# Layer-0 backward w1 blocks in four transfers each with sums in natural order, fewer output units inside the turn, and a new order of the last output units

## The chip, the cores and the metric

The kernel runs on one core of one Trainium2 chip. The metric is the device time of one execution in microseconds; the median of three runs before the change is 1110.19 us (1109.47 to 1112.6).

A core has five engines that run their own instruction streams in order and wait for each other on semaphores: PE (TensorE, matmuls), DVE (VectorE), ACT (ScalarE), POOL (GpSimd) and SP (SyncE). Here SP issues all loads from device memory, and the output row `out_1`; POOL issues nearly all stores. Sixteen DMA engines move the bytes for both.

## The reference

A decode step for a batch of 2 rows: two layers of grouped-query attention over a cached K and V of 16384 positions, each followed by an MLP, with the same weights in both layers, and the gradients of all inputs but `B_x`.

```python
def _A_ref(x, k_cache, v_cache, wq, wo):          # B=2, Hq=32, Hkv=4, Sk=16384, Dh=128, D=1024
    q = (x @ wq).reshape(B, Sq, Hq, Dh).transpose(0, 2, 1, 3)
    k, v = repeat(k_cache, 8, axis=1), repeat(v_cache, 8, axis=1)
    p = softmax(einsum("bhqd,bhkd->bhqk", q, k) * Dh ** -0.5)
    return einsum("bhqk,bhkd->bhqd", p, v).transpose(0, 2, 1, 3).reshape(B, Sq, Hq * Dh) @ wo
def _B_ref(x, w1, b1, w2, b2):                    # w1: 1024 x 3584, w2: 3584 x 1024
    return gelu(layernorm(x) @ w1 + b1) @ w2 + b2
x = x + _A_ref(layernorm(x), ...)                 # layer 0
x = x + _B_ref(layernorm(x), ...)
x = x + _A_ref(layernorm(x), ...)                 # layer 1, same weights
x = x + _B_ref(layernorm(x), ...)
# outputs: x and, by vjp(grad_out), the gradients of A_x, k_cache, v_cache, wq, wo, w1, b1, w2, b2
```

All tensors are bfloat16. K, V and their gradients are 32 MB each (8 pairs of batch row and KV head, 16384 x 128), `wq` and `wo` 8 MB each, `w1` and `w2` 7 MB each.

## The kernel before

K and V are read in pieces of 1 MB (32 positions of each of 128 partitions) and weights in blocks of 896 KB or 1 MB, into 16 slots of 1 MB in SBUF and a few regions that are free for a time. A recording layer (`Program`) collects the pieces of work in the order in which they are emitted, each with the chunks that it uses, and then places each load as early as a slot is free; so SP's queue holds the loads in the order of their first use, and a load waits there until the last reader of its slot is done. Each load also takes one of eight completion semaphores in turn, so that it waits until the load eight places ahead has landed.

The order of stages is: attention and MLP forward of layer 0, the same of layer 1, MLP backward of layer 1, attention backward of layer 1 (`attn_bwd(1, ...)`), **the turn** (MLP backward of layer 0), attention backward of layer 0 (`attn_bwd(0, ...)`), and **the end**. All large outputs are computed from the turn on: the weight gradients and the K and V gradients are outer products of a few rows, each unit of output being one matmul into a 128 x 512 PSUM bank, one cast into a staging slot by ACT or DVE (`cast_out`, L276 and L279), and after four or eight units one store from POOL's queue (L1333 for weights, 512 KB; L1257 for K and V, 1 MB).

The turn, by its emitted order (L1490 to L1530):

- `here_products` with w2 (PE L465, 224 matmuls) give dh; DVE multiplies it by the GELU slope (L1504), and `spread` (PE L506, DVE L507) lays it out for the products with w1.
- w1 comes in 8 blocks `ws1c` of 512 rows x 896 columns (`ld_rows`, L378), four row groups of 128 side by side in a partition: partition p of group j holds row 128j + p. `turn_rows` turns each block in 32 x 32 squares with two DVE instructions (L437). The list `t1` holds these 16 turns; its first two are placed in the last steps of `attn_bwd(1)`, the next two behind it, five between the products with w2, and the rest behind `spread`.
- `p1`, for each block 28 matmuls (PE L487), adds to `dm_0`, 128 x 16 in bank `sb[0]`. Because of the turning in squares the sums come out with partition groups of 32 and row groups exchanged, so that `unquad` copies them to natural order: one DVE copy out of PSUM (L517) and 16 copies of 32 partitions over DVE, ACT and POOL (L525 to L529, pattern `on="vag"`).
- Between the blocks of `p1` stand the first nine pieces of `first`: rows and columns for the w2 gradient (`y_rows`, `x_rows`) and its first six units. Six more units (`first[9:15]`) stand between the layer norm's sums (`g1p[0]`: DVE L649 to L652, PE L594) and the rest of it (`g1p[1]`: DVE L657 to L929).
- The result `gA_all` feeds the products with wo (PE L465, 64 matmuls) and `do_of`, after which `attn_bwd(0)` starts with its first V chunk (DVE L537).

`unquad` also serves `wo_bwd_ops` (three times in layer 0) and the MLP backward of layer 1; `dn_kept` and `dh_last_` call it with POOL alone.

In `attn_bwd`, `direct` adds the products of each K chunk to the query gradient in `sb[0][:, 0:8]` (PE L575); `dq_of` reads it out and clears it (L1052, L1054) once per position.

The end is written out by hand in `todo` (L1155 to L1158). What is left then: `dq_of` of the last position, 16 units and one turn (`turn`, PE L1233, copied at L1240 or L1243) of the last K gradient, a `y_rows`, eight groups of products with wq (`tail`, PE L465), the layer norm's backward (`sums` and `rest` in `attn_in_bwd`), the row `out_1` (L617 to L619), and 16 units of the wq gradient.

```python
todo = ev.pop(s) + kv_units[0:2] + rows + tail[0:4] + kv_units[2:4] + tail[4:] + units[0:2] + parts[0:1]
todo += units[2:5] + parts[1:2] + units[5:9] + parts[2:] + kv_units[4:] + units[9:]
```

Of the kernel before, what the change touches and what calls it, by code (L numbers as in the profile page):

```python
# [29 lines left out]
N_END = 133  # L30
# [152 lines left out]
def kernel(  # L183
# [24 lines left out]
    nc = tc.nc  # L208
# [38 lines left out]
    def flat(t):  # L247
        return t.rearrange("p a b -> p (a b)")
# [33 lines left out]
    def dve(us):  # L282
        load_of("dve", us)
# [92 lines left out]
    def ld_rows(nm, W, j0, rb, c0, n):  # L376
# [3 lines left out]
            W[j0 * 128:(j0 + rb) * 128, c0:c0 + n].rearrange("(j p) n -> p j n", p=128)), (nm, j0, c0))  # L380

    def ld_wq(k):
        return [ld_rows("wq", A_wq, 4 * i, 4, k * 1024, 1024) for i in range(2)]
# [128 lines left out]

    def unquad(dst, src, on="vag"):

        C = src.shape[1]
        q = small.tile([128, 8, 4, 2], F32, name="uq", bufs=1)[:, 0:C]
        V.tensor_copy(out=q, in_=src)  # L517
        n = 0
        for a in range(4):
            for j in range(4):  # L520
                d, s_ = dst[32 * a:32 * a + 32, :, j], q[32 * j:32 * j + 32, :, a]
                e = on[n % len(on)]
                n += 1
                if e == "v":
                    V.tensor_copy(out=d, in_=s_)  # L525
                elif e == "a":
                    S.copy(out=d, in_=s_)
                else:
                    GP.tensor_copy(out=d, in_=s_)  # L529
# [116 lines left out]

    def ln_bwd_sums(dy, y, at=None):
        t1 = wrk.tile([128, DJ, 2], F32, name="lb_t1")
        V.tensor_tensor(out=t1[:], in0=dy, in1=y, op=ALU.mult)  # L649
        s = small.tile([128, 2, 2], F32, name="lb_s")  # L650
        V.tensor_reduce(out=s[:, 0, :], in_=dy.rearrange("p j b -> p b j"), axis=AX.X, op=ALU.add)
        V.tensor_reduce(out=s[:, 1, :], in_=t1[:].rearrange("p j b -> p b j"), axis=AX.X, op=ALU.add)  # L652
        return part_sum(flat(s[:]), 4, at)

# [368 lines left out]

    def attn_bwd(l, order, gT, wo_first, outputs=None, mark=None, extra=None):

# [24 lines left out]
        def dq_of(pos, g):  # L1050
            def fn():
                V.tensor_scalar(out=dq_all[:, (g % HKV) * R:(g % HKV + 1) * R, 2 * l + g // HKV], in0=sb[0][:, 0:8],  # L1052
                                scalar1=QSCALE, scalar2=None, op0=ALU.mult)
                V.memset(sb[0][:, 0:8], 0.0)  # L1054
                dve(0.3)
            return fn
# [56 lines left out]
        while s <= n_steps:  # L1113
# [5 lines left out]
            for v in k_at.get(s, ()):  # L1119
                vpos, vi = divmod(v, 16)  # L1120
                vg = order[vpos]
                if vi % 4 == 0:
                    vc[0] = ld_kv("K", vg, vi // 4)
                c = vc[0]

                def pk(vpos=vpos, vg=vg, vi=vi, c=c):
                    direct(sb[0][:, 0:8], c, vi, xt[vpos % 2], False)

                mids.append((pk, [c]))
# [21 lines left out]
        if l == 1:  # L1151
            todo = tail + parts
        else:
            rows, kv_units, units = outputs(s, True)
            todo = ev.pop(s) + kv_units[0:2] + rows + tail[0:4] + kv_units[2:4] + tail[4:] + units[0:2] + parts[0:1]  # L1155
            todo += units[2:5] + parts[1:2] + units[5:9] + parts[2:] + kv_units[4:] + units[9:]
        for b in todo:
# [3 lines left out]
    def attn_in_bwd(l, gT, dnq):  # L1161
        h = {}

        def sums():
# [6 lines left out]
            h["dn"] = dn  # L1171
            h["ps"] = ln_bwd_sums(dn[:], vec_y[f"a{l}"][:], half[0, 0] if l == 1 else sb[0][:, 200:])
            dve(0.8)

        def rest():
# [6 lines left out]

        res = [(sums, ()), (rest, ())]
        if l == 0:
# [4 lines left out]
    def kv_outputs(pos, g):  # L1189
# [30 lines left out]
        for c, w in [(c, w) for c in range(NCH) for w in (1, 0)]:  # L1220
            at_ = base + 4 * c + 4 * (pos == 0) if w == 1 else base + 14 + 4 * c
            if w == 0 and pos == G - 1:
                at_ = (124, 127, N_END + 1, N_END + 3)[c]
            stg = P.chunk(kind="full")
# [21 lines left out]

            res.append((at_ - 2, turn, ()))
            for u in range(8):
# [229 lines left out]

    ws1c = [ld_rows("w1q", B_w1, 4 * h, 4, cg * 896, 896) for h in range(2) for cg in range(4)]
    dm_0 = quads(at_sb0(224, 16))  # L1480
    vh0, spread_h0 = spread(lambda: dh_all[:, :, 0:2], FJ, "vh")
# [7 lines left out]
    extra[30] = [col_to_row(xM1, out_0.rearrange("b s d -> (b s) d"), kind="load")]  # L1489
    attn_bwd(1, up, lambda: saved["g3"], (None, wo_prods), mark=mark("d1"), extra=extra)  # L1490
    wo_prods0 = wo_first_ops(0, down[0] % HKV, saved["wo"])[2]


    g2 = saved["gA1"]
    for b in t1[2:4]:
        emit(*b)
# [18 lines left out]
    first = [y_rows(gM_all, 0, 8, 0, 0)] + dw_units("h", 0, 0, pieces_rows(out_8, F, D))  # L1515
    rest_h = first[15:]
    for n, b in enumerate(p1):
        emit(*b)
        for u in first[n + (n > 0):n + 2]:
            emit(*u)  # L1520
    va0, spread_a0 = spread(lambda: gA_all[:, :, 0:2], DJ, "va")
    g1p = mlp_in_bwd(0, lambda dm: unquad(dm[:].rearrange("p (c j) b -> p c j b", j=4), dm_0), g2, parts=True)
    emit(g1p[0])
    emit(lambda: load_of("dve", 6.0))
    for u in first[9:15]:
        emit(*u)
# [93 lines left out]
```

## Time and profile before

| What | Before |
|---|---|
| median of 3 runs | 1110.19 us (1109.47 to 1112.6) |
| the profiled execution, its own time | 1110.15 us |
| its span from first to last instruction | 1108.4 us |
| mean granted TensorE clock | 0.821 |
| busy: PE, DVE, ACT, POOL | 815.9, 761.3, 493.1, 182.6 us (74%, 69%, 44%, 16%) |
| read, written | 349.20 MB, 98.62 MB |
| DMA busy share and rate, 675 to 730 us | 0.97, 375 GB/s |
| DMA busy share and rate, 730 to 1086 us | 1.02, 419 GB/s |
| DMA busy share and rate, 1086 to 1099 us | 0.49, 200 GB/s |

The spans of the stages are read from the timeline: the turn lies between about 641 us, when the last K chunk of layer 1's backward is used, and 675 us, when layer 0's attention backward turns its first V chunk; the last store is issued at 1099.59 us. The DMA share is the mean over the 16 engines of the time in which a packet was under way; it goes a little above 1 where packets overlap, so that 1.0 means that all sixteen always had work.

### The profile page before, as it was taken

Reading aid. Unit: us, or ns where it says so; the run is one execution under the profiler, and the core shown is the slowest. Engines: PE = TensorE matmul, PEld = TensorE weight load, DVE = VectorE, ACT = ScalarE, POOL = GpSimd, SP = SyncE. Lnnn points to the kernel's source line nnn. Section 1 sums busy time; section 2 is a strip of 40 time slices with the busy share of each in tenths; the row PEclk is TensorE's granted clock in tenths of the full one; section 3 lists DMA queues with packets and bytes.
Section 4 is the critical chain, followed back from the end, with each engine's and each line's share of the span. In section 5 each row is a group of like instructions: output and inputs, shape, how many; then the busy total and the mean of one; then the engine's idle time right before and its main releaser. Section 6 shows DMA issues by size and latency. Waiting matters only on the chain. (4 is left out here: it accounts for less than half of the span.)

```text
span 1108.4 us, 34192 instructions
## 1 busy us (share of the span) xinstructions
PE 815.9 (74%) x14689; PEld 609.3 (55%) x14689; DVE 761.3 (69%) x1474; ACT 493.1 (44%) x1133; POOL 182.6 (16%) x577
## 2 busy tenths in 40 slices
PE   5665666456888647888778678878876896698895
PEld 4554555455777547777677564444443443344453
DVE  5864665169888627665546476979776895598984
ACT  0322222102233222235434326767665785487874
POOL 1000000001000000111111101423332332233431
PEclk9999999997555555569868657999897998699998
DMA  9999999999999998999999989999999999999996
GB/s 372 421 422 421 422 425 421 398 404 399 418 423 421 422 421 345 409 419 421 419 423 416 417 318 411 355 399 422 420 420 425 423 419 422 420 402 421 410 423 250
DMA packets 97448, 450.03 MB, mean 406 GB/s; under 512 B 7528, under 2 KB 11638, under 8 KB 58512
## 3 DMA queue, kind: packets, MB, share of 16 engines
q1 hardware_dynamic: 79504, 349.22, 77.3%
q0 software_dynamic: 17792, 98.62, 21.6%
q8 instruction: 115, 1.88, 0.6%
q14 instruction: 37, 0.30, 0.1%
HBM read 349.20 MB, written 98.62 MB: 404 GB/s over the span
## 5 line engine op out<-in xcount | busy, mean ns | idle before, releaser
L537 DVE STREAM_TRANSPOSE kT<-slot 128x512 int32<-128x512 int32 x420 | 283.1, 694 | 112.8 <-PE sc L550 90.2
L550 PE MATMUL sc<-qbd,kT 128*128 128x32 bf16 x4096 | 262.5, 222 | 12.6 <-DVE kT L537 11.0
L550 PEld LDWEIGHTS <-kT 128*128 128x128 bf16 x4096 | 209.1, 115 | 64.7 <-issue 32.9
L575 PEld LDWEIGHTS <-slot 128*128 128x128 bf16 x3520 | 143.9, 103 | 106.7 <-issue 47.1
L575 PE MATMUL sb<-xt,slot 128*128 128x8 bf16 x3520 | 161.1, 176 | 49.0 <-DMA slot<-in_A_v_cache_dram 22.9
L276 ACT CAST slot<-sc 128x512 bf16<-128x512 f32 x293 | 167.0, 592 | 60.4 <-PE sc L1307 38.0
L1252 PE MATMUL sc<-slot,late 128*128 128x512 bf16 x350 | 131.1, 397 | 17.7 <-DVE slot L279 5.7
L279 DVE CAST slot<-sc 128x512 bf16<-128x512 f32 x171 | 114.3, 677 | 27.5 <-PE sc L1252 14.2
L760 ACT ACTIVATE e<-sc 128x512 bf16<-128x512 f32 x32 | 19.0, 597 | 235.9 <-DVE sc L757 169.0
L276 ACT CAST slot<-sb 128x512 bf16<-128x512 f32 x139 | 82.4, 593 | 37.1 <-PE sb L1307 17.0
L455 ACT COPY slot<-tp 128x512 int32<-128x512 int32 x88 | 50.3, 587 | 103.7 <-PE tp L452 103.4
L452 PE MATMUL tp<-ident,slot 128*128 128x128 bf16 x768 | 71.3, 255 | 13.2 <-ACT slot L455 6.0
L1252 PEld LDWEIGHTS <-late 128*128 128x128 bf16 x512 | 44.7, 98 | 62.2 <-issue 48.7
L585 ACT COPY xt<-e 32x128 int32<-32x128 int32 x256 | 75.6, 295 | 3.9
L1252 PE MATMUL sb<-slot,late 128*128 128x512 bf16 x162 | 65.6, 405 | 12.6 <-DVE slot L279 7.7
L1307 PE MATMUL sc<-slot,late 128*128 128x512 bf16 x159 | 64.0, 424 | 11.3 <-DVE e L279 6.2
L437 DVE STREAM_TRANSPOSE slot<-slot 128x1024 int32<-128x1024 int32 (+1 forms) x48 | 55.2, 1176 | 17.0 <-DMA slot<-in_A_wo_dram 8.0
L452 PEld LDWEIGHTS <-slot 128*128 128x128 bf16 x768 | 58.0, 116 | 15.9 <-issue 6.8
L279 DVE CAST slot<-sb 128x512 bf16<-128x512 f32 x81 | 54.9, 678 | 9.7 <-PE sb L1307 4.3
L642 POOL TENSOR_TENSOR m_rstd<-ln_vpe,neghalf 128x2 f32<-128x2 f32 x2 | 1.4, 715 | 349.6 <-DVE ln_vpe L640 349.6
L585 POOL COPY xt<-late 32x64 int32<-32x64 int32 x240 | 55.2, 230 | 13.0 <-DVE late L1046 1.9
L585 POOL COPY xt<-ds 32x64 int32<-32x64 int32 x128 | 29.5, 231 | 159.6 <-DVE ds L1046 104.7
(303 smaller groups left out, 1104.4 us busy)
## 6 DMA issues: line engine op xcount, KB each, us to landing
slot<-in_A_k_cache_dram SPq DMA_DIRECT2D x105, 1024.0 KB, 17.3
slot<-in_A_v_cache_dram SPq DMA_DIRECT2D x98, 1024.0 KB, 17.9
out_dram<-slot POOLq DMA_DIRECT2D x57, 1024.0 KB, 14.6
slot<-in_A_wq_dram SPq DMA_DIRECT2D x25, 1024.0 KB, 16.7
slot<-in_A_wo_dram SPq DMA_DIRECT2D x25, 1024.0 KB, 19.7
out_dram<-slot POOLq DMA_DIRECT2D x43, 512.0 KB, 13.9
slot<-in_B_w_dram SPq DMA_DIRECT2D x23, 896.0 KB, 15.4
slot<-in_B_w_dram SPq DMA_DIRECT2D x12, 1024.0 KB, 13.2
```

The source lines that it names most:

```text
L276: S.copy(out=dst, in_=src)
L279: V.tensor_copy(out=dst, in_=src)
L437: V.transpose(out=t.ap[:, h * nw * 256:(h + 1) * nw * 256].bitcast(I32).rearrange("p (w j m) -> p w j m", j=4, m=32), in_=c.ap[:, 0:4 * nc ...
L452: PE.transpose(tp[:, j * 128:(j + 1) * 128], c.ap[:, off + j * 128:off + (j + 1) * 128], ident[:])
L455: S.copy(out=d.bitcast(I32), in_=tp.bitcast(I32))
L537: V.transpose(out=kT[:].bitcast(I32).rearrange("p (w j m) -> p w j m", w=4, j=4), in_=c.ap[:, (i % 4) * 1024:(i % 4 + 1) * 1024].bitcast(I ...
L550: PE.matmul(sc[:, a0:a0 + 4, :, 2 * (i % 4) + q], lhsT=kv[:, 2 * q + w, :, e], rhs=qbd[:, q_at(g), 2 * w + e], start=(w == 0 and e == 0), ...
L575: PE.matmul(acc, lhsT=c.ap[:, n * 128:(n + 1) * 128], rhs=xv[:, i // 4, t // 2, :, 2 * (i % 4) + t % 2], start=(fresh and i == 0 and t == ...
L585: (GP.tensor_copy if on[t % len(on)] == "g" else S.copy)(out=d[32 * t:32 * t + 32, c0:c0 + cn, j, :], in_=s[32 * j:32 * j + 32, c0:c0 + cn ...
L760: S.activation(out=e_of(l, g)[:, 8 * f:8 * f + 8].rearrange("p a h b -> p h a b"), in_=sc[f][:].rearrange("p h (a b) -> p h a b", b=8), fu ...
L1252: PE.matmul(ps, lhsT=hold["blk"][:, j, :], rhs=flat(qm(w)[:, (u % 2) * 4:(u % 2) * 4 + 4, :]), start=True, stop=True)
L1307: PE.matmul(ps, lhsT=hold[j // 4 * 4][:, j % 4, :], rhs=Y.ap[:, y_at + c0:y_at + c0 + cn], start=True, stop=True)
```

## The change

It has five parts.

1. `ld_quads` takes the place of `ld_rows` for the eight w1 blocks of the turn: four transfers for each block, one for each row group j, each into all 128 partitions (1792 bytes a row, 224 KB). Partition 32a + r of group j now holds row 128a + 32j + r. On the memory side a transfer's access pattern is 4 x 32 x 896 (a, r, columns; strides 458752, 3584 and 1 elements), on the SBUF side 128 x 896; before, it was 128 x 4 x 896 on both sides. In the built program each transfer takes a completion semaphore of its own, and the order of SP's queue is otherwise as it was.
2. The sums then stand in natural order, and one DVE copy takes the place of `unquad` there. The other users of `unquad` get the pattern `vgvagvvg`: 8 copies on DVE, 6 on POOL, 2 on ACT, where it was 6, 5 and 5.
3. Two of the nine pieces of `first` stay inside `p1` (a `y_rows` behind the fourth block, an `x_rows` behind the sixth), and four units instead of six between the two parts of the layer norm. Eight units (two stores of 512 KB) move to the background of `attn_bwd(0)`. One turn of the second block moves ahead of layer 1's last layer norm (`mid`).
4. The query gradient of `attn_bwd` is added up in two places in turn, so that a position's products do not share the columns that the one before is read from.
5. At the end the last turn of the K gradient moves into the loop, the layer norm's sums are split from their matmul (`close`), and the units stand in another order.

```diff
+    def ld_quads(nm, W, j0, c0, n):
+
+        def load(ap):
+            src = W[j0 * 128:(j0 + 4) * 128, c0:c0 + n].rearrange("(a j r) n -> j a r n", a=4, j=4)
+            for j in range(4):
+                nc.sync.dma_start(ap[:, j * n:(j + 1) * n], src[j])
+
+        return P.chunk(load, (nm, j0, c0))
...
-    def unquad(dst, src, on="vag"):
+    def unquad(dst, src, on="vgvagvvg"):
...
-    def ln_bwd_sums(dy, y, at=None):
+    def ln_bwd_terms(dy, y):
...
-        return part_sum(flat(s[:]), 4, at)
+        return flat(s[:])
+
+    def ln_bwd_sums(dy, y, at=None):
+        return part_sum(ln_bwd_terms(dy, y), 4, at)
...
-                V.tensor_scalar(out=dq_all[:, (g % HKV) * R:(g % HKV + 1) * R, 2 * l + g // HKV], in0=sb[0][:, 0:8],
+                acc = sb[0][:, pos % 2 * 8:pos % 2 * 8 + 8]
+                V.tensor_scalar(out=dq_all[:, (g % HKV) * R:(g % HKV + 1) * R, 2 * l + g // HKV], in0=acc,
                                 scalar1=QSCALE, scalar2=None, op0=ALU.mult)
-                V.memset(sb[0][:, 0:8], 0.0)
+                V.memset(acc, 0.0)
...
-                    direct(sb[0][:, 0:8], c, vi, xt[vpos % 2], False)
+                    direct(sb[0][:, vpos % 2 * 8:vpos % 2 * 8 + 8], c, vi, xt[vpos % 2], False)
...
-            todo = tail + parts
+            todo = tail + list(mid) + parts
...
-            todo = ev.pop(s) + kv_units[0:2] + rows + tail[0:4] + kv_units[2:4] + tail[4:] + units[0:2] + parts[0:1]
-            todo += units[2:5] + parts[1:2] + units[5:9] + parts[2:] + kv_units[4:] + units[9:]
+            todo = ev.pop(s) + kv_units[0:4] + rows + kv_units[4:6] + tail[0:4] + kv_units[6:8] + tail[4:] + kv_units[8:10]
+            todo += parts[0:1] + units[0:4] + parts[1:2] + units[4:8] + parts[2:3] + kv_units[10:13] + parts[3:]
+            todo += kv_units[13:] + units[8:]
...
-            h["ps"] = ln_bwd_sums(dn[:], vec_y[f"a{l}"][:], half[0, 0] if l == 1 else sb[0][:, 200:])
+            h["s"] = ln_bwd_terms(dn[:], vec_y[f"a{l}"][:])
             dve(0.8)
+
+        def close():
+            h["ps"] = part_sum(h["s"], 4, half[0, 0] if l == 1 else sb[0][:, 200:])
...
-        res = [(sums, ()), (rest, ())]
+        res = [(sums, ()), (close, ()), (rest, ())]
...
-                at_ = (124, 127, N_END + 1, N_END + 3)[c]
+                at_ = (124, 127, N_END + 1, N_END + 2)[c]
...
-            res.append((at_ - 2, turn, ()))
+            res.append((min(at_ - 2, N_END - 1), turn, ()))
...
-    ws1c = [ld_rows("w1q", B_w1, 4 * h, 4, cg * 896, 896) for h in range(2) for cg in range(4)]
-    dm_0 = quads(at_sb0(224, 16))
+    ws1c = [ld_quads("w1q", B_w1, 4 * h, cg * 896, 896) for h in range(2) for cg in range(4)]
+    dm_0 = at_sb0(224, 16).rearrange("p (c a b) -> p c a b", a=4, b=2)
...
-    attn_bwd(1, up, lambda: saved["g3"], (None, wo_prods), mark=mark("d1"), extra=extra)
+    attn_bwd(1, up, lambda: saved["g3"], (None, wo_prods), mark=mark("d1"), extra=extra, mid=t1[2:3])
...
-    for b in t1[2:4]:
+    for b in t1[3:4]:
         emit(*b)
...
-    rest_h = first[15:]
+    rest_h = first[6:]
     for n, b in enumerate(p1):
         emit(*b)
-        for u in first[n + (n > 0):n + 2]:
-            emit(*u)
+        if n in (3, 5):
+            emit(*first[n // 4])
...
-    g1p = mlp_in_bwd(0, lambda dm: unquad(dm[:].rearrange("p (c j) b -> p c j b", j=4), dm_0), g2, parts=True)
+    g1p = mlp_in_bwd(0, lambda dm: V.tensor_copy(out=dm[:], in_=dm_0.rearrange("p c a b -> p (c a) b")), g2, parts=True)
...
-    for u in first[9:15]:
+    for u in first[2:6]:
         emit(*u)
```

More of the change, by code (lines that the diff above doesn't have):

```diff
@@ L1022, in wq_last_ops, with attn_bwd @@
         return turns, prods
-    def attn_bwd(l, order, gT, wo_first, outputs=None, mark=None, extra=None):
+    def attn_bwd(l, order, gT, wo_first, outputs=None, mark=None, extra=None, mid=()):
         kvs = []
```

## The prediction

> **What bounds the kernel now.** I read the stages' DMA share first, then the DMA issues and packets, then the timelines of the turn and of the end.
>
> ```profile
> 642.00:645.00 3.00, 1.94 (x53) 1.79 (x51) 0.86 (x6) 0.00 (x0) 0.52 (x1) 0.50 1.04 388
> ...
> 660.00:663.00 3.00, 3.00 (x84) 2.41 (x82) 2.25 (x3) 1.72 (x3) 0.00 (x0) 0.50 0.09 33
> ...
> 730.00:1086.00 356.00, 291.95 (x3545) 157.61 (x3545) 280.60 (x481) 248.78 (x496) 118.16 (x349) 0.92 1.02 419
> ```
>
> The last three columns of these windows are granted clock, DMA share and GB/s. Over most of the span the sixteen DMA engines are full at about 420 GB/s; what is lost is lost in gaps, such as 660 to 663 us inside the turn (33 GB/s). So an edit is worth what it takes from a gap, and a new gap costs its full length. While the w1 blocks land (642 to 645) the engines are full too, at 388 GB/s.
>
> ```profile
> DMA packets 97448, 450.03 MB, mean 406 GB/s; under 512 B 7528, under 2 KB 11638, under 8 KB 58512
> ## 3 DMA queue, kind: packets, MB, share of 16 engines
> q1 hardware_dynamic: 79504, 349.22, 77.3%
> ```
>
> ```profile
> e<-in_A_x_dram SPq DMA_DIRECT2D x1, 4.0 KB
> ds<-in_grad_out_dram SPq DMA_DIRECT2D x1, 4.0 KB
> ds<-in_B_b_dram SPq DMA_DIRECT2D x1, 7.0 KB
> slot<-in_B_b_dram SPq DMA_DIRECT2D x1, 2.0 KB
> ```
>
> These tell on how many engines a transfer of SP's queue runs. By the list of issues the queue carries 239 K and V chunks of 128 rows, 73 weight blocks of 512 rows (wq 31, wo 28, w2 14), 16 forward w1 blocks of 128 rows, 8 w1 blocks of 512 rows for the turn, and five small transfers with 2, 2, 1, 1 and 2 rows (the four shown and the row `out_1`). One packet a row makes 30592 + 37376 + 2048 + 4096 + 8 = 74120. The queue has 79504; the other 5384 are exactly 336 x 16 + 8. So each of the 336 large transfers, whose outermost dimension is 128, has 16 extra packets, and the five small ones have 8, which is their rows 2+2+1+1+2. I read the extra packet as one completion for each engine that took part: a transfer uses no more engines than its outermost dimension has entries.
>
> ```profile
> 660.18 2.11 DVE L437 STREAM_TRANSPOSE slot<-slot 128x896 int32<-128x896 int32 x2
> 665.38 0.17 DVE L517 COPY uq<-sb 128x16 f32<-128x16 f32 x1 [3.09 <-PE sb L487]
> 665.59 1.04 DVE L525 COPY dm_sb<-uq 32x4 f32<-32x4 f32 x6
> 667.53 0.17 DVE L649 TENSOR_TENSOR lb_t<-dm_sb,m_y 128x16 f32<-128x16 f32 x1 [0.90 <-ACT dm_sb L527]
> ...
> 675.09 1.27 DVE L537 STREAM_TRANSPOSE kT<-slot 128x512 int32<-128x512 int32 x2
> ```
>
> This is the chain of the turn: the last block's turning, its products on PE (waited for 3.09 us), the copying to natural order, the layer norm, the first V chunk.
>
> **The change part by part.**
>
> *The four transfers.* On the SBUF side each has 128 entries outermost, as all large ones have; on the memory side it has 4. The trace has no transfer whose sides differ. A part that one engine moves must be cut on both sides, and a cut along the outermost dimensions that both share gives four parts; so I take four engines. The bounds are 16 engines (no loss) and four. [...]
>
> One transfer on four engines gives each 57344 bytes, as much as a whole block gives each of sixteen, so it takes what a block took.
>
> ```profile
> slot<-in_B_w_dram SPq DMA_DIRECT2D x1, 896.0 KB, 10.7
> ...
> slot<-in_B_w_dram SPq DMA_DIRECT2D x1, 896.0 KB, 12.3
> ```
>
> These are the second and third block, issued at 631.55 and 632.18 us by SP's timeline: landed at 642.25 and 644.48, 2.2 us apart; 917504 bytes at the 388 GB/s of the window above are 2.36. I take 2.3 us (bounds 2.18, at 420 GB/s, and 2.45, at 375). The first block landed at 637.5 (issued 625.24, 12.3). Now three steps more: 644.4. Behind it stands a K chunk, 2.5 us: 646.9. Then 28 transfers, 64.4 us: the last lands at 711.3, where it was 656.1 (649.60 + 6.5). Only eight may be under way, but all eight stand on the same four engines (18 us of work), so SP's issues (0.38 us each, 32 for 8) and waits are hidden behind them; twelve engines idle. SP's later loads are queued behind these. Turning the last block takes 2.11 us, its 28 products 0.94 (PE L487 in the timeline): the sums are read at 714.4 instead of 665.38, +49.0. In between, the half-turn moved into `mid` makes DVE wait for the second block (landing at 656), and with it the last layer norm of layer 1 and the w2 products; all of that ends before 670 and hides behind the loads. With 16 engines it costs nothing, as DVE idles 1.94 us there.
>
> *Natural order.* From L517 to L649 were 2.15 us; one copy of 0.17 and its hand-over leave 0.2: -1.95. It is on the chain in either case.
>
> *Fewer units.* Seven units less among the products would let them end with the turning (below, 3.0 us); behind the loads this is worth nothing. Four units instead of six behind the sums: PE came to the wo products at 671.03, while `gA_all` was written at 670.21: -0.8. Eight units and two stores (1 MB) move into attention backward: 2.5 us at 419 GB/s where the engines are full, nothing where they fill the 6 us that 675 to 730 loses at 375 GB/s: +1.2 (0 to 2.5).
>
> The first V chunk is turned 49.0 - 1.95 - 0.8 = 46.2 us later. Loads behind it: two V chunks are issued near 695, behind the blocks, and land within 5 us of 711; the third waits for all four transfers into its slot and for the turning, 713.4, and lands 5.0 later (as the one issued at 662.32 did), long before the twelve-odd us of work on the first two are done: 0 (to +5).
>
> *The other `unquad` users*: two DVE copies more (0.17 each), three ACT copies fewer (0.2), three times in a stage that loads bound: 0 (-1 to +1). *Two accumulators*: PE spares a wait of at most 0.4 us per position, behind the same loads: 0 (-1).
>
> *The end.*
>
> ```profile
> 1095.40 0.57 POOL L1257 DMA_DIRECT2D out_dram<-slot  x1 [2.41 <-ACT slot L276]
> ...
> 1099.59 0.74 POOL L1333 DMA_DIRECT2D out_dram<-ds  x1 [0.48 <-issue]
> ```
>
> From the clearing of the last accumulator (1083.66) to the last cast (1099.03) are 15.4 us, for 32 casts of 0.69 on DVE and 0.59 on ACT: 10.2 us side by side. DVE's other work (out-row, layer norm, 3.5) and ACT's row (1.0), shared, add 2.25: 12.4. The first K store, at 1095.40, now needs only units that stand ahead of the norm, so fewer stores queue behind each other at the end. -3 (0 to -5).
>
> Sum: 1110.15 (the profiled execution; the median, 1110.19, is the same) + 46.2 + 1.2 - 3 = **1154.5 us**.
>
> **The rivals.**
>
> *Sixteen engines after all*, or different fours for successive transfers: the SBUF side alone decides, for it the 128 partitions speak; against it, nothing in the trace but the reading above. SP issues two loads back to back 0.44 us apart (652.26 and 652.70), a transfer takes 0.57, so the rate holds. Then the last block's products start with its turning's end, 0.85 earlier because `mid` takes a turn off DVE: they end at 662.4 instead of 665.38, -3.0, and with -1.95 and -0.8 the chain gains 5.75. Of this the moved stores give back up to 2.5 and full loads from 730 on some more: -3.5. With the end's -3: **1103.6**, faster. It decides if the first block lands near 637.5.
>
> *Sixteen engines, but too few bytes under way.* Eight transfers of 224 KB are 1.79 MB; if each takes the 6.5 us from issue to landing that the last block took, plus 0.4 for the issue, the rate is 266 GB/s instead of 388, and 7.34 MB take 27.6 us instead of 18.9: +8.7. With the gains (-5.8, -3) and +1.2 for the stores: **1111.3**. Against it: a chunk issued into an empty queue (662.32) landed after 5.0 us, 2.5 of which are its own bytes.
>
> **How the numbers follow.** Four engines 0.80, sixteen 0.13, too few under way 0.07. Four engines alone span 31 steps at 2.18 to 2.45 (-3.7, +4.7), the stores, the late V chunk (+5), the end (-2, +3) and, downwards, gaps behind the turn that a delayed stage may fill (675 to 730 and 1086 to 1099 lose 6 us each): 1139 to 1168. The two rivals lie below it and hold 2 in 10. This kernel's runs scatter by 0.3%, so less than 3.3 us is no change. Faster: 0.11 of the first rival's 0.13. No change: the rest of it and half of the second, 0.05. Slower: 0.84.
>
> **What would show it.** With four engines the windows between 650 and 710 us show a DMA share of a quarter and some 100 GB/s, DVE L437 waits for the w1 loads for tens of us, and SP's queue has 79504 - 128 + 32 x 4 = 79504 packets again; with sixteen it has 79888. The first V chunk is turned near 721. L517 is gone from the turn, and L649 follows the copy by 0.2 us. At the end a K store is issued near 1088 plus the delay. I am wrong if the first block lands near 637, as before.

## The result and the profile after

| | before | after |
|---|---|---|
| median, runs of one job | 1110.68 us (1109.47 to 1112.6, 5 runs) | 1167.17 us (1166.57 to 1168.54, 5 runs) |
| the profiled execution, its own time and span | 1110.15 and 1108.4 us | 1166.57 and 1164.8 us |
| mean granted TensorE clock | 0.821 | 0.821 |

After takes 1.051 times as long as before (95% interval 1.0499 to 1.0522): +56.5 us, where +44.3 was forecast (1154.5 less 1110.19). 1167.17 lies inside the predicted range of 1139 to 1168, near its upper end.

Three windows of the trace of after. The columns are the window and its length, the busy time and (behind an x) the instructions of PE, PE's weight loads, DVE, ACT and POOL, then granted clock, DMA share and GB/s.

```profile
644.00:647.00 3.00, 1.02 (x32) 0.95 (x33) 1.29 (x4) 0.00 (x0) 0.00 (x0) 0.50 0.26 101
650.00:700.00 50.00, 13.48 (x410) 12.58 (x410) 13.56 (x24) 3.26 (x3) 0.00 (x0) 0.50 0.27 102
776.00:1145.00 369.00, 299.04 (x3608) 161.45 (x3606) 288.90 (x500) 253.86 (x499) 120.97 (x356) 0.94 1.01 415
```

While w1 lands, a quarter of the DMA engines' time is used and 102 GB/s are moved; before it was 388 GB/s in the window of the prediction, and 355 GB/s from 637 to 652 us. Later all sixteen are full again, at 415 GB/s. The page's lines on packets have the counts of before:

```profile
DMA packets 97448, 450.03 MB, mean 386 GB/s; under 512 B 7528, under 2 KB 11638, under 8 KB 58512
...
q1 hardware_dynamic: 79504, 349.22, 74.1%
```

That SP's queue has 79504 packets once more, with 24 more transfers, is the sign that the prediction named: 8 transfers with 16 extra packets each went, 32 with 4 each came.

The timelines of SP's queue and of DVE in after, through the turn:

```profile
637.21 61.65 SPq L387 DMA_DIRECT2D slot<-in_B_w_dram  x26
698.96 14.70 SPq L373 DMA_DIRECT2D slot<-in_A_v_cache_dram  x4
```

```profile
710.72 2.11 DVE L446 STREAM_TRANSPOSE slot<-slot 128x896 int32<-128x896 int32 x2 [8.78 <-DMA slot<-in_B_w_dram]
713.46 0.17 DVE L1539 COPY dm_sb<-sb 128x16 f32<-128x16 f32 x1 [0.63 <-PE sb L496]
713.66 0.17 DVE L658 TENSOR_TENSOR lb_t<-dm_sb,m_y 128x16 f32<-128x16 f32 x1
...
720.70 1.86 DVE L546 STREAM_TRANSPOSE kT<-slot 128x512 int32<-128x512 int32 x3
```

```profile
DVE slot L446 <- DMA slot<-in_B_w_dram: 51.7, 7, 9.2
```

SP issues 26 of the 32 transfers in 61.65 us; the later ones follow each other by 2.19 us: in the program each waits for the transfer eight places ahead, and 229376 bytes at the 102 GB/s of the window are 2.25. DVE waits for them seven times, 51.7 us in all (the last line: total, how often, longest), as the prediction said. The last block is turned at 710.72 (before 660.18), its sums are copied at 713.46 (before 665.38, +48.1), the layer norm follows 0.20 us behind, and the first V chunk is turned at 720.70 (before 675.09): +45.6.

The end of after, from POOL's timeline:

```profile
1147.93 0.53 POOL L1274 DMA_DIRECT2D out_dram<-slot  x1 [5.84 <-ACT slot L276]
...
1157.74 0.72 POOL L1350 DMA_DIRECT2D out_dram<-ds  x1 [0.49 <-issue]
```

The last store is issued at 1157.74 instead of 1099.59. So the delay grows from +45.6 at the first V chunk to +58.1 there, and is +56.4 at the end of the span. Read along the turnings of the K and V chunks (DVE L546, before L537), it is +47.2 at the 9th, +53.5 at the 17th, +53.2 still at the 24th from the end, and +57.8 at the 16th from the end.

One more point of the traces orders what follows. The third V load of layer 0 (in e11 the second) is the first load that goes into a slot out of which a w1 block was turned; SP issues it right behind the last block's turning (710.72 + 2.11 = 712.83 in after), and five more loads follow within 4 us. I call it **the late load**. SP's timelines of before and of after have it at 662.32 and 712.86 us (+50.5):

```profile
662.32 0.33 SPq L373 DMA_DIRECT2D slot<-in_A_v_cache_dram  x1
```

```profile
712.86 0.33 SPq L373 DMA_DIRECT2D slot<-in_A_v_cache_dram  x1
```

From it to the end of the span the kernels here move 179 MB (e11 180), which is 426 us at 420 GB/s (419 in before from 730 to 1086 us); the rest of that **stretch** is roughly what the DMA engines lose in it.

| kernel | what differs | late load, us | stretch, us | median (its range), us |
|---|---|---|---|---|
| before | | 662.3 | 446.1 | 1110.61 to 1111.51 in the jobs |
| after | | 712.9 | 451.9 | 1167.17 |
| e1 | after, 32 outermost, groups of 32 partitions | 676.5 | 452.8 | 1132.72 (1131.08 to 1136.37) |
| e2 | after, 8 outermost | 682.6 | 452.4 | 1136.62 (1136.41 to 1137.06) |
| e3 | after, units in the turn | 715.3 | 444.8 | 1161.12 (1159.24 to 1162.1) |
| e4 | before, new end | 664.0 | 446.6 | 1110.75 (1109.79 to 1112.46) |
| e5 | after, loads and sums of before | 663.7 | 455.5 | 1117.69 (1115.68 to 1121.02) |
| e6 | e5, four transfers by row groups | 664.1 | 453.2 | 1120.05 (1119.08 to 1123.64) |
| e7 | e5, four transfers by groups of 32 partitions | 678.9 | 458.2 | 1132.02 (1129.35 to 1138.88) |
| e8 | after, clearing on DVE | 713.8 | 451.8 | 1166.90 (1166.72 to 1167.43) |
| e9 | after, rate of before | 714.0 | 449.9 | 1165.74 (1164.77 to 1166.52) |
| e10 | e5, rate of before | 662.9 | 450.0 | 1115.13 (1110.35 to 1117.71) |
| e11 | e5, six staging halves | 662.3 | 449.5 | 1112.22 (1111.09 to 1113.57) |
| e12 | e5, units in the turn | 663.6 | 445.7 | 1110.76 (1108.69 to 1111.72) |

The late load and the stretch are of the profiled execution. In e4, e5, e7 and e11 that was the longest one, 1.8, 3.3, 6.9 and 1.4 us above the median, so that the two columns together are too long there by as much. Kernels with the same turn (after, e8, e9) have the late load at 712.9 to 714.0, so a difference of 1 us in that column means nothing.

### The profile page after: what moved, and what is told of

It is laid out like the page before. It is cut to its first block, busy times and chain, and to the rows that moved or that the text cites. A ratio compares the mean times of both kernels' runs of the same rounds, so it can differ in the third digit from the quotient of the medians.

```text
span 1164.8 us, 34252 instructions
## 1 busy us (share of the span) xinstructions
PE 816.7 (70%) x14689; PEld 610.6 (52%) x14689; DVE 763.9 (66%) x1480; ACT 488.0 (42%) x1112; POOL 182.4 (16%) x576
## 3 DMA queue, kind: packets, MB, share of 16 engines
q1 hardware_dynamic: 79504, 349.22, 74.1%
## 5 line engine op out<-in xcount | busy, mean ns | idle before, releaser
L546 DVE STREAM_TRANSPOSE kT<-slot 128x512 int32<-128x512 int32 x420 | 282.9, 694 | 107.9 <-PE sc L559 87.6
L276 ACT CAST slot<-sc 128x512 bf16<-128x512 f32 x274 | 156.6, 593 | 39.8 <-PE sc L1324 19.0
L1269 PE MATMUL sc<-slot,late 128*128 128x512 bf16 x336 | 126.7, 400 | 31.5 <-DVE slot L279 11.2
L279 DVE CAST slot<-sc 128x512 bf16<-128x512 f32 x182 | 121.4, 676 | 34.4 <-PE sc L1324 12.0
L276 ACT CAST slot<-sb 128x512 bf16<-128x512 f32 x154 | 91.1, 592 | 65.3 <-PE sb L1324 40.7
L446 DVE STREAM_TRANSPOSE slot<-slot 128x1024 int32<-128x1024 int32 (+1 forms) x48 | 55.4, 1177 | 59.5 <-DMA slot<-in_B_w_dram 51.7
L1269 PE MATMUL sb<-slot,late 128*128 128x512 bf16 x176 | 70.3, 400 | 8.2 <-DVE slot L279 3.9
L1324 PE MATMUL sc<-slot,late 128*128 128x512 bf16 x172 | 65.0, 404 | 7.8 <-DVE slot L279 4.0
L1350 POOL DMA_DIRECT2D out_dram<-slot x50 | 33.1, 663 | 154.1 <-DMA slot<-in_A_v_cache_dram 69.0
L279 DVE CAST slot<-sb 128x512 bf16<-128x512 f32 x70 | 47.6, 679 | 12.5 <-PE sb L1269 6.8
```

Of the source, the lines that this page charges most:

```text
L276: S.copy(out=dst, in_=src)
L279: V.tensor_copy(out=dst, in_=src)
L446: V.transpose(out=t.ap[:, h * nw * 256:(h + 1) * nw * 256].bitcast(I32).rearrange("p (w j m) -> p w j m", j=4, m=32), in_=c.ap[:, 0:4 * nc ...
L546: V.transpose(out=kT[:].bitcast(I32).rearrange("p (w j m) -> p w j m", w=4, j=4), in_=c.ap[:, (i % 4) * 1024:(i % 4 + 1) * 1024].bitcast(I ...
L1269: PE.matmul(ps, lhsT=hold["blk"][:, j, :], rhs=flat(qm(w)[:, (u % 2) * 4:(u % 2) * 4 + 4, :]), start=True, stop=True)
L1324: PE.matmul(ps, lhsT=hold[j // 4 * 4][:, j % 4, :], rhs=Y.ap[:, y_at + c0:y_at + c0 + cn], start=True, stop=True)
```

## The experiments

### What slows the loads: e1, e2, e6, e7

All four keep 32 transfers of 224 KB and the other parts of the change.

**e1**, partition groups in place of row groups, so that both sides have 32 outermost:

```diff
-            src = W[j0 * 128:(j0 + 4) * 128, c0:c0 + n].rearrange("(a j r) n -> j a r n", a=4, j=4)
-            for j in range(4):
-                nc.sync.dma_start(ap[:, j * n:(j + 1) * n], src[j])
+            src = W[j0 * 128:(j0 + 4) * 128, c0:c0 + n].rearrange("(a j r) n -> a r j n", a=4, j=4)
+            for a in range(4):
+                nc.sync.dma_start(ap[32 * a:32 * a + 32, 0:4 * n].rearrange("p (j n) -> p j n", j=4), src[a])
```

> The changed kernel, with each w1 block of the turn again in four transfers of 224 KB, sums in natural order, but cut by partition groups of 32 instead of row groups: each transfer's outermost dimension is 32 on both sides. Theory F (the outermost 4 of the memory side holds a transfer to four DMA engines): the step goes from the 2.19 us measured after the change to 0.5 to 0.6 us, the first block lands near 637.5 us, SP's queue shows 79888 packets, the windows of the turn show a DMA share near 1 again. Rival T (four small transfers for each block are slow in themselves, by too few bytes under way): the first V chunk is still turned after 678 us. On the 12 us that the changed kernel loses behind the turn: if they come from loads that start late behind the blocks (theory L), they go too, and the time is 1102 to 1108 us; if they come from the eight units and two stores moved behind the turn (theory U), they stay, and it is 1112 to 1119 us.

Measured 1132.72 us: neither of the two times. The first V chunk is turned at 684.36, behind the 678 us that rival T gave as its sign. Packets and a window, of the page and the trace of e1:

```profile
q1 hardware_dynamic: 79888, 349.22, 77.5%
```

```profile
655.00:670.00 15.00, 10.19 (x345) 9.86 (x345) 10.88 (x12) 1.90 (x1) 0.00 (x0) 0.50 1.08 235
```

All sixteen engines take part (79888 packets) and are busy all the time (share 1.08), but they move 235 GB/s; SP issues the transfers some 1.0 us apart, not the 0.5 to 0.6 expected. So the count of engines was right and was not all that matters. Whether the number of the transfers, their rows or their partitions slow them was open.

**e2**, eight outermost on the memory side:

```diff
-            src = W[j0 * 128:(j0 + 4) * 128, c0:c0 + n].rearrange("(a j r) n -> j a r n", a=4, j=4)
+            src = W[j0 * 128:(j0 + 4) * 128, c0:c0 + n].rearrange("(a j r) n -> j a r n", a=8, j=4)
```

> The changed kernel, with the memory side of the four transfers 8 x 16 x 896 instead of 4 x 32 x 896: the same bytes, the same row length, the same 128 partitions, but rows reach other partitions, so the gradients behind these products are computed from permuted sums. Theory F: eight engines, a step of 1.10 us (half of 2.19), a DMA share near a half while the blocks land, SP's queue 79504 + 32 x 4 - 0 completions less than with sixteen, that is 79632 packets; the turn ends about 16 us later than with sixteen engines (51 us x (35 - 19) / (70 - 19)), so the time is 1116 to 1128 us. If the slowness comes from the row groups or the strides and not from the count, the step stays near 2.2 us and the time near 1165 us.

Measured 1136.62 us, outside the forecast, with the mechanism as theory F has it:

```profile
q1 hardware_dynamic: 79632, 349.22, 76.1%
```

```profile
650.00:665.00 15.00, 7.08 (x241) 6.87 (x238) 8.01 (x18) 1.90 (x1) 0.03 (x1) 0.50 0.53 201
```

79632 packets, a share of half, 201 GB/s, twice the 102 of four; by that rate a transfer of 229376 bytes takes 1.14 us, where theory F had 1.10. The time was off because I added the longer turn to about 1104 us. Added to the time of the kernel with the loads and sums of before (e5, 1117.69), the delay of the late load (682.6 - 663.7 = 18.9) gives 1136.6; e5 is known to about 2 us only, so that it fits so well is in part chance. Since e2's rows reach other partitions, its gradients are other numbers, and only its time and its trace are used here.

**e6**, four transfers by row groups in the row order of before, 128 outermost on both sides (sums by `unquad` again, as in e5):

```diff
-            src = W[j0 * 128:(j0 + 4) * 128, c0:c0 + n].rearrange("(a j r) n -> j a r n", a=4, j=4)
+            src = W[j0 * 128:(j0 + 4) * 128, c0:c0 + n].rearrange("(j p) n -> j p n", j=4)
```

> As e5, but each w1 block in four transfers of 224 KB, one for each row group of 128 rows, all partitions (128 x 896 on both sides): the number, the size and the partitions of the changed kernel's transfers, without the 4 on the memory side. Theory F (the outermost 4 is what costs): the time of e5 within 3 us, the blocks land at 380 GB/s or more, SP's queue shows 79504 + 24 x 16 = 79888 packets. Rival T (four transfers of 224 KB for each block are slow in themselves, as e1 with its 1.0 us steps could mean): the blocks land at 230 to 300 GB/s, and the time is that of e5 plus 8 to 20 us.

Measured 1120.05 us, 2.4 above e5, whose range it overlaps; the late load comes 0.4 us later than in e5. SP's queue in the timeline of e6, and a window while the blocks land:

```profile
636.14 17.04 SPq L387 DMA_DIRECT2D slot<-in_B_w_dram  x25
```

```profile
642.00:657.00 15.00, 8.96 (x297) 8.56 (x294) 10.50 (x21) 1.90 (x1) 0.52 (x1) 0.50 1.00 358
```

25 transfers in 17.0 us where after had 26 in 61.65, and SP's queue has the 79888 packets of sixteen engines. 358 GB/s are less than the 380 that theory F had, but before and e5 move no more from 642 to 657 us (344 and 348). So four transfers of 224 KB for a block cost next to nothing; rival T falls, and with it the prediction's "too few bytes under way". With the same number, size and partitions, only the memory side with its 4 outermost is left to explain after; that it is their number is what e2 shows, where 8 in place of 4 double the rate (201 GB/s instead of 102).

**e7**, as e6, but cut by groups of 32 partitions:

```diff
+            for a in range(4):
+                nc.sync.dma_start(ap[32 * a:32 * a + 32, 0:4 * n].rearrange("p (j n) -> p j n", j=4), src[32 * a:32 * a + 32])
```

> As e5, but each w1 block in four transfers of 224 KB, one for each group of 32 partitions (32 x 4 x 896 on both sides), rows in the order of before. In e1 such transfers used all sixteen engines but moved only 231 to 251 GB/s. Theory N (a transfer into 32 partitions alone is slower for each packet, whatever the rows): 230 to 260 GB/s while the blocks land with a DMA share near 1, a step of 0.9 to 1.1 us, 1128 to 1138 us. If the slowness of e1 came from its row order (rows 32 apart in one partition), the blocks land at 380 GB/s or more and the time is that of e5.

Measured 1132.02 us, and in a window of e7:

```profile
657.00:672.00 15.00, 10.25 (x346) 9.91 (x346) 10.68 (x11) 1.90 (x1) 0.00 (x0) 0.50 1.07 236
```

Theory N holds: 236 GB/s, as in e1, with the row order of before. e1 has its sums in natural order by one copy and e7 by `unquad`, and the two times (1132.72 and 1132.02) show no gain of natural order; but with ranges of 5 and 10 us they could not show the 2 us of the prediction either.

### What is lost behind the turn: e3, e5, e8 to e12

**e3**, the units of the w2 gradient back in the turn:

```diff
-    rest_h = first[6:]
+    rest_h = first[15:]
...
-        if n in (3, 5):
-            emit(*first[n // 4])
+        for u in first[n + (n > 0):n + 2]:
+            emit(*u)
...
-    for u in first[2:6]:
+    for u in first[9:15]:
```

> The changed kernel, four transfers with outermost 4 kept, but the units of the w2 gradient back inside the turn as before the change (nine pieces among the products, six units between the two parts of the layer norm). Theory U (the moved units and their two stores cost the 12 us that are lost behind the turn): 1153 to 1157 us, and the shift of the K and V turnings against the kernel before stays near 46 to 48 us. Theory L (the loads held back behind the last block are late, the moved stores add only their bytes): 1162 to 1168 us, the shift still grows past 53 us.

Measured 1161.12 us, between the two. The late load comes 2.5 us later than in after and 1.3 later than in e9 (715.3); what of that the units in the turn cost is not shown. The delay is +48.9 at the first V chunk and +52.8 at the 17th turning, so that the 17th is hardly earlier than in after (+53.5), as theory L says. But from there on it does not grow (+50.6 at the 16th from the end), and the stretch is 444.8 us, 7.1 less than in after. Both theories held half: in e3 the start of the stage is as late as the late load (+52.8 at the 17th turning, +53.0), and without the moved units the stretch is as short as before.

**e5**, the loads and the sums of before:

```diff
-    ws1c = [ld_quads("w1q", B_w1, 4 * h, cg * 896, 896) for h in range(2) for cg in range(4)]
+    ws1c = [ld_rows("w1q", B_w1, 4 * h, 4, cg * 896, 896) for h in range(2) for cg in range(4)]
...
```

> The changed kernel with the loads and the sums of before: one transfer of 896 KB for each w1 block (128 x 4 x 896 on both sides) and the copying to natural order by 17 copies; the fewer units in the turn, the two accumulators and the new end stay. It prices parts 3 to 5 of the change at full load speed. The prediction's terms (nothing in the turn beyond a few us of gain, +1.2 for the moved units, -3 at the end) give 1104 to 1109 us. Theory L (behind the turn the loads set the time: the shift after the first position's start is that of the first V load issued behind the last block's turning, plus 3 to 4 us, whatever the turn gained), with the 4 to 6 us that e1 and e2 lost later in the stage, and -1 to -3 at the end, gives 1112 to 1117 us, with the first V chunk turned near 670 us and the shift at the 17th block of that stage near +3 all the same.

Measured 1117.69 us, ratio to before 1.0053 (1.0036 to 1.007): even without `ld_quads` the change makes the kernel a little slower, 4 to 8 us. That is above what the prediction's terms give, and 0.7 us above the range of theory L. The first V chunk is turned at 673.05, 2.0 us earlier than before; at the 17th turning the delay is +5.3. What lies between is in DVE's timeline of e5, and in DVE's waits from 663 to 863 us:

```profile
695.30 0.69 DVE L279 CAST slot<-sb 128x512 bf16<-128x512 f32 x1 [0.27 <-issue]
699.25 0.69 DVE L279 CAST slot<-sc 128x512 bf16<-128x512 f32 x1 [3.26 <-DMA out_dram<-slot]
```

```profile
DVE slot L279 <- DMA out_dram<-slot: 5.8, 2, 3.3
```

In the second line a cast into a staging half has to wait 3.26 us until the store that last read this half has landed (the waits give the total, how often, and the longest); behind it on DVE stand the turnings of the V chunk and the casts of the other units, behind these SP's next load (in after SP's K and V loads wait 50 times for such a turning over the span, 159.0 us in all). The same wait takes 4.33 us at 743.8 us in after. In the trace of e12, where the units are in the turn, these waits add up to 0.7 us from 663 to 863 us.

**e12**, e5 with the units back in the turn, the edit of e3.

> As e5, but the units of the w2 gradient back inside the turn; what stays of the change is the two accumulators, the turn of the second block ahead of layer 1's norm, the copying pattern and the new end. If the moved units are the whole of e5's loss, 1109 to 1112 us, no difference to before that the measurement can tell; if the rest of the change costs something, 1114 to 1119 us; by the prediction's terms (-3 for the end, 0 for the rest) 1106 to 1108 us.

Measured 1110.76 us, ratio 0.9992 (0.9983 to 1.0001): the time of before. So the two accumulators, the turn ahead of the norm, the copying pattern and the new end cost and gain nothing together that shows, and moving the units costs 1117.69 - 1110.76 = 6.9 us (1167.17 - 1161.12 = 6.1 with the slow loads). By the interval of e5 such a difference is good to about 2 us.

**e11**, e5 with more staging:

```diff
-HALF_AT = (-1, -1, 18)
+HALF_AT = (-1, -1, -1)
```

> As e5, with the rate of e5, but six staging halves instead of four in the first 18 steps of the last attention stage (one slot less for loads there). If the lack of staging buffers is what loses the time behind the turn, 1110 to 1114 us; if it is the rate or the order alone, 1116 to 1120 us; if the slot that the loads lose counts more, above 1120 us.

Measured 1112.22 us, 5.5 less than e5, ratio to before 1.0006 (0.9997 to 1.0015). The 25 us that begin 15 us behind the late load, in the windows of before, e5 and e11:

```profile
677.30:702.30 25.00, 22.74 (x239) 11.85 (x237) 19.80 (x33) 19.73 (x41) 7.51 (x22) 0.91 0.98 399
```

```profile
678.70:703.70 25.00, 18.94 (x191) 9.51 (x188) 15.64 (x25) 16.92 (x35) 8.07 (x23) 0.91 0.82 327
```

```profile
677.30:702.30 25.00, 21.70 (x228) 10.82 (x227) 19.30 (x33) 19.57 (x41) 8.60 (x24) 0.98 1.02 413
```

In e5 the DMA engines are at 0.82 there and DVE does 25 instructions instead of 33; with two staging halves more they are at 1.02 and DVE does 33 again. In after the same window (727.9 to 752.9) has 0.82 as well. That the moved units lose their time for want of staging buffers is shown for this much of it.

**e9** and **e10**, after and e5 with the weight units let in at the rate of before:

```diff
-            state["credit"] += max(1.3, len(bg) / (120 - s)) if s < 116 else 3
+            state["credit"] += max(1.3, (len(bg) - 9 * (s < 40)) / (120 - s)) if s < 116 else 3
```

> The changed kernel, four engines and moved units, but up to step 40 of the last attention stage the weight units are let in at the rate of before (the eight units and one x-row piece more are not counted in the rate until then). From the issue of the first V load behind the turn to the end all kernels move 179 MB; it takes 446 us before, 445 us with the units in the turn (e3), 452 us in the changed kernel, and the windows show the difference as idle DMA engines 15 to 40 and 60 to 100 us behind that load. Theory S (the moved units raise the rate at which weight units ask for the few staging buffers of the first steps, and a cast that waits for a store to land holds all of DVE): the stretch takes 445 to 448 us and the time is 1160 to 1163.5 us. If the rate is not it, the time is 1165 to 1168 us.

> As e5 (w1 blocks and sums as before, the other parts of the change kept) with the rate of e9. Theory S: 1110 to 1113.5 us instead of e5's 1117.7. If the rate is not it: 1116 to 1119 us.

Measured 1165.74 and 1115.13 us: 1.4 and 2.6 us less than after and e5. Both are above what theory S had, and e9 lies where it was to lie if the rate is not it. Two windows of e9, the 25 us that begin 15 us behind its late load and a later stretch, tell more:

```profile
729.00:754.00 25.00, 21.39 (x225) 11.05 (x223) 19.37 (x33) 18.65 (x38) 8.62 (x24) 0.93 0.97 387
1072.00:1096.00 24.00, 21.78 (x242) 11.35 (x241) 21.73 (x36) 18.33 (x35) 5.26 (x8) 0.93 0.89 324
```

In the first place theory S holds: the DMA share is 0.97 instead of after's 0.82, and DVE does 33 instructions instead of 25. In the 200 us behind the late load the waits of casts for stores are 1.9 us in all instead of 7.1 (e10 1.8, e11 2.1, e5 5.8), and the delay at the 17th turning is +49.2 instead of +53.5 (e10 -0.6, e5 +5.3). But units that are let in later have to be done later. Between the 24th and the 16th turning from the end the delay grows by 9.7 us in e9 and in e10, where it grows by 4.7 in after and 5.9 in e5 and e11; in e9 that begins at 1048 us, and the second window lies at its end, with 324 GB/s where after moves 398 from 1070.9 to 1094.9 us. So the rate takes away the first loss as two more halves do, and most of the time is lost again near the end; what holds the units up there was not tried.

**e8**, the clearing on DVE:

```diff
-                GP.memset(Xt[b][:], 0.0)
+                V.memset(Xt[b][:], 0.0)
```

It follows these lines of after, from the timelines of POOL, DVE and PE:

```profile
1063.58 4.30 POOL L594 COPY xt<-late 32x64 int32<-32x64 int32 x16
1067.83 0.57 POOL L1274 DMA_DIRECT2D out_dram<-slot  x1
1068.43 0.52 POOL L1302 MEMSET late<- 128x512 bf16 x1
```

```profile
1068.99 0.42 DVE L271 COPY late<-sc 4x512 bf16<-4x512 bf16 x1 [4.92 <-POOL late L1302]
```

```profile
1069.47 0.58 PE L1269 MATMUL sc<-slot,late 128*128 128x512 bf16 x1 [4.29 <-DVE late L271]
```

> The changed kernel, four engines and all, with one edit: the clearing of the x-row buffers (128 x 512, 0.52 us on POOL) is done by DVE. In the changed kernel one such clearing stood on POOL behind the 4.3 us of the exchange copies and behind a store, and DVE waited 4.9 us and PE 4.3 us for it near 1065 us, where the shift against before grew from 53.2 to 57.8 us; before the change that did not happen. Theory X (the units moved into this stage put the clearing behind the exchange): the step of the shift there is gone and the time is 1161 to 1164 us. If the DMA engines, which were full in that stretch, set the time all the same, it stays within 1.5 us of the changed kernel's 1167.2.

Measured 1166.90 us, as after. The step is gone (the delay is +51.8 instead of +57.8 at the 16th turning from the end, the last K load comes 6.6 us earlier), and nothing is gained: from the last K load to the last store it takes 43.8 us instead of 39.0, and the stretch stays at 451.8. The window of after says why such a wait is a poor sign:

```profile
1063.40:1073.40 10.00, 5.59 (x48) 2.58 (x48) 3.98 (x8) 3.48 (x8) 4.85 (x19) 0.83 1.02 421
```

PE, DVE and ACT stand still for 4 to 5 us, but the DMA share is 1.02: the engines that bound this stage had work throughout. Theory X was wrong about the time. What held the end of e8 in place of it was not tried.

### The end: e4

Before with the new order of the end alone (the lines of part 5 in the diff above).

> The kernel before with only the new order of the end. The prediction's term: -3 us (0 to -5), so 1105 to 1110 us, with the time from the last K load's issue to the last store's issue shorter than 40.9 us by 2 to 4. If part of the growth of the shift at the last position (53.2 to 59.4 us) comes from the new order, the last kT turnings are late here too, and the time is 1111 to 1115 us.

Measured 1110.75 us, ratio 0.9998 (0.9989 to 1.0008). The first of the last two K stores is issued at 1090.47, where it was 1095.40 (29.3 us behind the last K load instead of 36.7), and the last store 39.1 us behind the last K load, where it was 40.9. But from the last K load to the end of the span it takes 49.4 us against 49.7: the stores are issued sooner and the span ends no sooner. The order of the end is worth nothing that shows here.

## Why the prediction was right, and what it missed

| step of the prediction | forecast | measured | by |
|---|---|---|---|
| four engines: the sums are read later | +49.0 | +48.1; in the time +49.5 | 713.46 less 665.38; after less e5 (late load +49.2) |
| natural order, fewer units behind the sums | -2.75 | -2.5 up to the first V chunk; in the time none that shows | 7.24 us instead of 9.71; e1 against e7 |
| eight units and two stores moved | +1.2 | +6.1 to +6.9 | after less e3, e5 less e12 |
| other users of `unquad`, accumulators, `mid` | 0 | 0 with the end | e12 against before |
| the end | -3 | 0 | e4 |
| sum of the times | +44.4 | +55.6 to +56.4 | after less before: +56.5 |

The sum of the measured column is no check of its own: after less e5, e5 less e12 and e12 less before are steps from one kernel to the next, and add up by construction.

**The four engines** were right in kind and size. The step was taken as 2.3 us and measured 2.19, the last block's sums came at 713.46 instead of 714.4. Outermost sizes of 4, 8 and 32 beside 128, 128 and 32 gave 4, 8 and 16 extra packets a transfer, which the prediction read as one for each engine, and shares of 0.27, 0.53 and 1.08. Before has no large load whose sides differ, so that four engines were the author's inference there; after and e2 show it for unlike sides.

**The rivals with sixteen engines** are out for this kernel, but their prices were too low: e5 and e6, the change at full load speed but for the natural order, take 1117.69 and 1120.05 us, not 1103.6 or 1111.3, because the gains of the turn and of the end did not show in the time and the moved units cost more. (The second rival's 1.79 MB are 1.84 MB; its 266 GB/s are worked out with that.) Four transfers in natural order on all engines and into all partitions were not run; natural order gained nothing that shows in e1, so nothing here speaks for a time below that of before.

**The moved units** are the term that was mis-sized: +1.2 (0 to 2.5) by their bytes at full DMA rate, +6.1 to +6.9 measured. The price was taken from the bytes alone. What it left out is that a unit needs a staging half, that the first steps of the stage have four halves for all weight units and for the repeated q rows, and that a cast which waits for a store to land holds DVE for everything behind it (3.26 us in e5, 4.33 in after). Two more halves give back 5.5 us of e5's loss (e11). The measured cost is about 4 us beyond this term's own bound of 2.5. That the time still lies inside the range, 0.8 us below its top, is in part luck: the 4.7 us that were kept above for slower steps made room for it, and the steps came out faster than taken.

**The gains within the turn** came where they were forecast: the first V chunk at 720.70 against 721.3, 7.24 us behind the sums (8.07 in e3, with six units there, so that the -0.8 for fewer units came too). They were not carried into the time. The prediction put the step "the third V chunk late" at 0 (to +5). But the first V chunk was turned 7.8 us behind the late load instead of 12.8, and the loads behind that one came no sooner; in e3 the delay at the 17th turning is that of the late load (+53.0 there, +52.8), not that of the first chunk (+48.9). So part of the bound of +5 belonged in the sum. How much is not told apart: in after the delay at the 17th turning is 3 us above that of the late load, and in e9 (+51.7, +49.2), e10 and e11 it is 1 to 3 us below, so that the late load alone does not set it and the moved units have a share.

**The end** was forecast at -3 by counting casts on DVE and ACT; the last store was issued 1.8 us sooner behind the last K load (e4), and the span ended no sooner. Its sign came all the same: in after the first of the last two K stores is issued at 1147.93, near 1088 plus the delay of 58.

## What to carry to other kernels

The engines of SP's transfers followed from the outermost sizes of both sides here (4, 8 and 16 engines for 4, 8 and 32 or more; beside 128 in SBUF, 4, 8 and 128 in memory moved 102, 201 and 358 GB/s); before a load is split or reordered, multiply out the pattern on the memory side, and read the result from the packet count and the DMA share. In a stage that the DMA engines bound (here with a share of 1.01 to 1.02), date everything from the first load that waits for the stage before: in these runs work that ended sooner without moving that load gained nothing that shows (the first V chunk of after is turned 7.8 us behind it instead of 12.8), and what left DMA engines idle behind it cost time (e5, at a share of 0.82 there, takes 5.5 us more than e11 at 1.02). Work moved into such a stage can cost more than its bytes, by the buffers it needs there (here 6.1 to 6.9 us where the bytes are 2.5); none of the versions tried here beat the kernel before by more than can be told from no change.

## What the runs showed of the hardware that was not expected

Transfers into 32 partitions use all sixteen engines, which then show a share of 1.07 to 1.08, yet 235 to 236 GB/s are moved (e1, e7), against 358 GB/s for e6's transfers of the same size into 128 partitions, with a share of 1.00. A busy DMA share is therefore not the full rate. Why transfers into 32 partitions are slower, no run here shows.
